# Two groups of attention stages per step on TensorE, and three tiles moved between PSUM banks

## The chip, the core and the metric

The kernel runs on one core of one Trainium2 chip. A core has TensorE (PE, matrix multiplication, and PEld, the loading of its weights), VectorE (DVE), ScalarE (ACT), GpSimd (POOL) and SyncE (SP, which issues the DMAs). Each engine works through its own queue in order and waits on semaphores for the others. TensorE writes into PSUM, which has eight banks; ScalarE and VectorE read it from there. The metric is the time on the device in microseconds, the median of several runs.

## The reference

Linear attention with random features (FAVOR), and then a gated MLP over its output. Eight batches, eight heads, 576 rows, a head size of 64, 128 features; the MLP has 4608 rows, a model width of 512 and an inner width of 1536.

```python
def phi(x):
    proj = einsum('bhsd,md->bhsm', x, omega)
    h = proj - sum(x * x, axis=-1) / 2.0
    h = h - max(h, axis=-1)
    return exp(h) / sqrt(m)
q_p, k_p = phi(q * scale), phi(k * scale)
kv  = einsum('bhsm,bhsd->bhmd', k_p, v)
z   = sum(k_p, axis=2)
num = einsum('bhsm,bhmd->bhsd', q_p, kv)
den = einsum('bhsm,bhm->bhs', q_p, z)[..., None] + 1e-06
x   = (num / den)  # heads side by side: 4608 x 512
g   = x @ w_gate
out = (g / (1 + exp(-g)) * (x @ w_val)) @ w_out
```

## The kernel before, in words

**Attention.** The work is cut into groups of 256 rows of a pair of heads. A group is a block of q or of k, and a step takes two groups: the first six steps take two of k, the next sixty one of q and one of k, the last six two of q, 72 steps (0 to 71). The stages of one group are spread over several steps. `load` (L340) brings q and k three steps ahead. `st_transpose` (L363) turns both groups into the tile `pt` with four TensorE transposes, and ScalarE copies it to `x` (L378), one step ahead. `st_project` (L382) multiplies `x` by omega into two banks, `pp0` and `pp1`. `st_max` (L399) takes the maxima on VectorE (L411 to L414), and `st_exp` (L417) the exponentials on ScalarE, eight instructions (L425), into `ph`. `k_accumulate` (L510) sums k's features times v into `kvacc`, two steps later, in two halves; a sum that is complete is copied to `kvr` (L441), and from batch 4 on its row of denominators is transposed into `zp` (L447). `q_transpose` (L543) turns q's features into `ptq`, copied to `qt` (L554). For batches 0 to 3, `q_mult` (L556) multiplies by `kvr` into `po` and divides by the denominator on VectorE, and `q_out` (L592), three steps behind, transposes the result into `xt`. For batches 4 to 7 the denominators come from GpSimd and VectorE (`q_den`, L471), GpSimd divides the features (`q_norm`, L497), and `q_out` multiplies straight into `xt`. ScalarE and VectorE then split `xt` into a high and a low part, `xh` (L626) and `xl` (L627).

**The MLP** is a generator, `stream` (L683). It goes over 40 visits, each a tile of 512 (or 256) rows of x with a set of three of the twelve blocks of 128 inner columns. A visit is three `g` (L641, 12 matmuls each), then the `o` of the visit before (L650, nine matmuls for each 128 rows), then three `v` (L641). Every product is made of three matmuls from high and low parts. ScalarE applies Silu to `g` (L707), VectorE multiplies by `v` (L721), ScalarE and GpSimd split the result (`hh` L724, `hl` L725), and VectorE adds `o` to the sum (L674). Weights are converted beforehand by another generator, `convert_all` (L247), a `tick` at a time, and loaded again and split for each set (L242, L243).

**The order.** A loop over the steps (L776) calls the eleven stages of `ORDER` (L754). After each stage it gives out some of the MLP, `give(due / left)`, and some ticks of the conversion, so that both keep to a plan: `course` (L191) says how much of the MLP is to be done by which step, within what x allows. The MLP can begin at step `EARLY`, which is 21, when the first two tiles of x are whole. `DENSE` is 35, the step by which all weights are to be converted. The framework then puts the instructions of each engine into a queue by its own estimate of when operands and buffers are ready, earlier emitted work first, and sets the semaphores.

**The banks.** `ps_moe` has four banks for `g`, `v` and `o`; `ps_proj` has two, for `pp0` and `pp1`; `kvacc` has one. The eighth, `ps_att`, is shared in turn by `ptq`, `po`, `xt`, `zp` and, from step 35 on, `pt`; before that `pt` takes a bank of the MLP. In the first 21 steps, which have no MLP work yet, `ptq` and every second `pp` take the MLP's banks too.

Of the kernel before, what the change touches and what calls it, by code (L numbers as in the profile page):

```python
# [23 lines left out]
def kernel(  # L24
# [16 lines left out]
    P = 128  # L41
# [5 lines left out]
    G = 256  # L47
# [23 lines left out]
    OLAG = 3  # L71
# [19 lines left out]
    def ps_att(name, shape):  # L91
        return ps_a.tile(shape, F32, name=name, tag="b")
# [27 lines left out]
    def slots(n, kind):  # L120

        if not 0 <= n < NS:
            return []
        return [(i, b, g, (kgroups if kd == "k" else qgroups)[g]) for i, (kd, b, g) in enumerate(steps[n]) if kd == kind]

    def pairs_of(gr):
        return [(2 * c, 2 * c + 1) for c in range(CH)] if gr is None else [gr[:1]] * CH
# [3 lines left out]
    def column(b, gr):  # L131
        return b * S + (S - RES if gr is None else gr[1])
# [10 lines left out]
    def tile_of(col):  # L143
        j = max(j for j, (c, _) in enumerate(TILES) if c <= col)
        return j, col - TILES[j][0]
# [45 lines left out]
    course = (lower + upper) / 2  # L191
# [8 lines left out]
    EARLY = whole[1]  # L200
# [5 lines left out]
    DENSE = marks[-1][0]  # L206
# [73 lines left out]
    ticks = [0]  # L280

    def tick():
        ticks[0] += 1
        next(wa, None)
# [55 lines left out]
    def load(n):  # L340
        if n >= NS:
            return
        nats[n] = att.tile([P, 2, CH, 2, D], F32, name=f"nat{n}", tag="nat", bufs=3)
        for kind, src in (("q", q), ("k", k)):
            for i, b, _, gr in slots(n, kind):
                load_group(nats[n][:, i], src, b, gr, False)
# [16 lines left out]
    def st_transpose(n):  # L363
        if n >= NS:
            return
        nat = nats.pop(n)
        pt = (ps_moe if n < DENSE else ps_att)(f"pt_{n}", [P, 2, G])
        for i in range(2):
            for c in range(CH):
                nc.tensor.transpose(  # L370
                    pt[:, i, c * P : (c + 1) * P], nat[:, i, c].rearrange("p h d -> p (h d)"), ident
                )
        x = att.tile([P, 2, G], F32, name=f"x_{n}", tag="x")

        st = att.tile([P, 4, 2, CH, 2], F32, name=f"st_{n}", tag="st", bufs=6)
        sq = att.tile([P, 2, CH, 2, D], F32, name=f"sq_{n}", tag="sq")
        nc.gpsimd.tensor_tensor(sq, nat, nat, op=ALU.mult)  # L377
        nc.scalar.copy(x, pt)  # L378
        sts[n] = x, st, sq
        return True  # L380
# [57 lines left out]
    def kv_finalize(b, a2):  # L438
        acc = kvacc.pop((b, a2))
        raw = att.tile([P, 4, VW], F32, name=f"kvr{b}_{a2}", tag="kvr", bufs=4)  # L440
        nc.scalar.copy(raw, acc)  # L441
        for j in range(2):
            kvst[b, 2 * a2 + j] = raw[:, 2 * j : 2 * j + 2, :]
        if b >= BPOOL:

            zp = ps_att(f"zp{b}_{a2}", [4, P])
            nc.tensor.transpose(zp, raw[:, :, D], ident)  # L447
            zs = att.tile([4, P], F32, name=f"zs{b}_{a2}", tag="zs")
            nc.scalar.copy(zs, zp)
            zd = dram.tile([4, P], F32, name=f"zd{b}_{a2}", tag="zd", bufs=4)  # L450
            nc.sync.dma_start(zd, zs)
            zds[b, a2] = zd
# [44 lines left out]
    def q_norm(n):  # L497
        n -= NLAG
        for _, b, g, gr in slots(n, "q"):
            if b < BPOOL:  # L500
                continue
            dn = dns.pop((b, g))
            phv = box["q", b, g].rearrange("p c (h m) -> p (c h) m", m=M)
            nc.gpsimd.tensor_tensor(
                phv, phv,
                dn[:, 2].rearrange("p c (h o) -> p (c h) o", o=1).broadcast_to([P, 2 * CH, M]),
                op=ALU.mult,
            )

    def k_accumulate(n, half):  # L510

        n -= KLAG
        ks = [(b, g, gr, c) for _, b, g, gr in slots(n, "k") for c in range(CH)]
        for b, g, gr, c in ks[half * len(ks) // 2 : (half + 1) * len(ks) // 2]:
            ph, vt = box["k", b, g], vrows[b, g]
            if c == CH - 1:
                busy.remove(vt)
                del box["k", b, g]
            for j, pr in enumerate(pairs_of(gr)[c]):
                a2 = pr // 2  # L520
                first = (b, a2) not in kvacc
                if first:
                    kvacc[b, a2] = ps_k.tile([P, 4, VW], F32, name=f"kvacc{b}_{a2}", tag="kv")
                acc = kvacc[b, a2]
                done.setdefault((b, a2), []).append(pr)
                last = LAST[pr] == (g, c)
                for hh in range(2):
                    nc.tensor.matmul(  # L528
                        acc[:, 2 * (pr % 2) + hh, :],
                        ph[:, c, hh * M : (hh + 1) * M],  # L530
                        vt[:, 2 * c + j if gr is None else c, hh, :],
                        start=first and hh == 0,
                        stop=last,
                        skip_group_check=True,
                    )
                if len(done[b, a2]) == NACC:
                    kv_finalize(b, a2)
        return bool(slots(n, "k"))
# [50 lines left out]
    xt = {}  # L589
    cols_done = [0]  # L590

    def q_out(n):  # L592
        n -= OLAG
        for _, b, g, gr in slots(n, "q"):
            po = ps_att(f"xt{b}_{g}", [P, G])
            first = column(b, gr)
            if b < BPOOL:
                xn = xns.pop((b, g))
                for c in range(CH):
                    nc.tensor.transpose(po[:, c * P : (c + 1) * P], xn[:, c].rearrange("p h d -> p (h d)"), ident)  # L600
            else:
                qt = qts.pop((b, g))

                segs = [(pr, pr * RES, RES) for pr in range(NPAIR)] if gr is None else [(gr[0], 0, G)]
                for pr, o, w in segs:
                    for hh in range(2):
                        nc.tensor.matmul(  # L607
                            po[hh * D : (hh + 1) * D, o : o + w], kvst[b, pr][:, hh, 0:D], qt[:, hh, o : o + w],
                            start=True, stop=True, skip_group_check=True,
                        )  # L610
            j, o = tile_of(first)
            if gr is None:
                parts_ = [(po.rearrange("d (r c) -> d r c", c=RES), slice(0, NPAIR), j, o, RES)]
            else:
                cut = min(TILES[j][1] - o, G)
                parts_ = [(po[:, 0:cut], gr[0], j, o, cut)]
                if cut < G:
                    parts_.append((po[:, cut:G], gr[0], j + 1, 0, G - cut))
            for src, pr, j, o, w in parts_:
                if j not in xt:  # L620

                    while j - NXB >= 0 and not finished(j - NXB):
                        assert give(1), "the MLP waits for x, and x for the MLP"
                    xt[j] = [xres.tile([P, NPAIR, T], F32R, name=f"x{e}{j}", tag=f"x{e}") for e in "hl"]
                hi, lo = (t[:, pr, o : o + w] for t in xt[j])
                nc.scalar.copy(hi, src)  # L626
                nc.vector.tensor_tensor(lo, src, hi.bitcast(F32), op=ALU.subtract)  # L627
            if gr is None or gr[0] == NPAIR - 1:
                cols_done[0] = first + (RES if gr is None else G)
        return bool(slots(n, "q"))  # L630
# [23 lines left out]
    def finished(j):  # L654

        return at_visit[0] > last_visit[j]
# [80 lines left out]
    debt = [0.0]  # L737
    given = [0.0]

    def give(us):  # L740
        debt[0] += us
        while debt[0] > 0:
            u = next(ma, None)
            if u is None:
                debt[0] = 0.0
                return False
            debt[0] -= u
            given[0] += u
        return True
# [1 line left out]

    ORDER = (  # L754
        st_project,
        q_norm,
        q_out,
# [5 lines left out]
        lambda n: k_accumulate(n, 1),  # L763
        st_exp,
        q_den,
    )

    for n in range(2):
# [7 lines left out]
    for n in range(NN):  # L776
        load(n + LA)
        load_v(n + LAV)
        want = OPS * np.interp(clock[n + 1], [clock[m] for m, _ in marks], [x for _, x in marks])
        for i, what in enumerate(ORDER):  # L780
            left = len(ORDER) - i
            what(n)
            due = course[n + 1] - given[0] - debt[0]
            if due > 0:
                give(due / left)
            for _ in range(int(np.ceil((want - ticks[0]) / left))):
                tick()
        load_z(n)
    for _ in ma:
        pass  # L790
# [30 lines left out]
```

## Time and profile before

| what | value |
|---|---|
| median of three runs | 1264.08 us (1259.43 to 1271.75) |
| the profiled execution | 1261.98 us |
| its span from the first to the last instruction | 1260.2 us |
| mean granted clock of TensorE | 0.986 |
| TensorE busy | 1222.5 us (97%) |
| ScalarE, VectorE, GpSimd busy | 632.5, 526.1, 506.2 us |
| first MLP matmul, last transposed x | about 107 and 1035 us |

The page of a profile gives each engine's busy time; a group of instructions by line, operation and tile; and what an engine waited for. `xl<-xt,xh` means that an instruction writes tile `xl` from `xt` and `xh`. A wait is written as the waiting engine, line and tile, an arrow, and the one that released it. Matmuls overlap, so the time that one costs is read from the distance between two starts and not from its duration. The granted clock is the share of TensorE's full clock that it was given.

### The profile page before, as it was taken

What the parts mean: (1) busy time and instruction counts of PE and PEld (TensorE: products, weight loads), DVE (VectorE), ACT (ScalarE), POOL (GpSimd) and SP (SyncE); (2) the same over time, 40 slices, a digit from 0 to 9 for tenths busy, and PEclk for the clock granted to TensorE, in tenths of its full rate; (3) what the DMA queues carried; (4) which work ended last, traced back from release to release, by engine and by line L of the source; (5) the groups of instructions that cost most, each with busy time, mean ns of one, the idle gap of its engine ahead of it and who ended that gap; (6) DMA issues with size and microseconds to landing.
All of it is one profiled execution on the core that took longest, in us unless ns stands there. A gap on an engine that the chain in (4) does not pass through costs nothing.

```text
span 1260.2 us, 19027 instructions
## 1 busy us (share of the span) xinstructions
PE 1222.5 (97%) x7137; PEld 1004.1 (80%) x7137; DVE 526.1 (42%) x1080; ACT 632.5 (50%) x1368; POOL 506.2 (40%) x448
## 2 busy tenths in 40 slices
PE   6999999999899999999999999999999999999998
PEld 5888878888688878877777777877777778888887
DVE  4886795557732343334433433223343311121112
ACT  4887857564444645555556644853644323221211
POOL 3344444445442212644544334444654314242421
PEclk7999999999999999999999999999999999999999
DMA  6656555344521222222212221221211111010112
GB/s 161 152 139 154 141 146 172 106 137 122 159 67 52 61 65 60 76 67 62 65 51 67 68 59 38 64 65 45 52 50 30 39 25 50 25 51 25 51 30 55
DMA packets 157692, 97.80 MB, mean 78 GB/s; under 512 B 119680, under 2 KB 132000, under 8 KB 157600
## 3 DMA queue, kind: packets, MB, share of 16 engines
q1 hardware_dynamic: 157600, 96.59, 28.7%
q8 instruction: 56, 0.92, 0.3%
q14 instruction: 36, 0.29, 0.1%
HBM read 77.66 MB, written 18.89 MB: 77 GB/s over the span
## 4 chain that ended last, share of the span: by engine, by line
PE 67%; DVE 2%; POOL 2%; issue 1%; ACT 1%; DMA 0%; POOLq 0%; ACTq 0%
PE o L650 20%; PE g L641 19%; PE v L641 17%; PE pp L393 3%; PE kvacc L528 2%; PE ptq L552 2%; PE pt L370 2%; PE xt L607 1%; POOL jk L488 1%; PE po L569 1%; ACT ph L425 1%; DVE st L411 1%; DVE dj L492 0%; POOL wlo L243 0%; POOL hl L725 0%
## 5 line engine op out<-in xcount | busy, mean ns | idle before, releaser
L725 POOL TENSOR_TENSOR hl<-sl,hh 128x512 fp32r<-128x512 f32 (+1 forms) x120 | 145.3, 1211 | 223.0 <-ACT hh L724 222.9
L243 POOL TENSOR_TENSOR wlo<-wraw,whi 128x512 fp32r<-128x512 f32 x108 | 138.5, 1294 | 146.1 <-ACT whi L242 135.4
L425 ACT ACTIVATE ph<-pp,st 128x128 f32<-128x128 f32 x576 | 167.7, 387 | 57.7 <-DVE st L414 56.9
L641 PE MATMUL g<-xh,whi 128*128 128x512 f32 (+1 forms) x480 | 185.4, 387 | 0.0
L641 PE MATMUL v<-xh,whi 128*128 128x512 f32 (+1 forms) x480 | 184.3, 384 | 0.0
L641 PE MATMUL g<-xh,wlo 128*128 128x512 f32 (+1 forms) x480 | 179.8, 375 | 0.0
L641 PE MATMUL v<-xh,wlo 128*128 128x512 f32 (+1 forms) x480 | 179.3, 374 | 0.0
L641 PE MATMUL g<-xl,whi 128*128 128x512 f32 (+1 forms) x480 | 179.2, 373 | 0.0
L641 PE MATMUL v<-xl,whi 128*128 128x512 f32 (+1 forms) x480 | 178.5, 372 | 0.0
L650 PE MATMUL o<-whi,hh 128*128 128x512 f32 x432 | 176.5, 408 | 0.6 <-DVE sl L721 0.6
L650 PE MATMUL o<-whi,hl 128*128 128x512 f32 x432 | 169.9, 394 | 1.1 <-POOL hl L725 0.6
L650 PE MATMUL o<-wlo,hh 128*128 128x512 f32 x432 | 170.3, 394 | 0.0
L724 ACT CAST hh<-sl 128x512 fp32r<-128x512 f32 (+1 forms) x120 | 70.0, 583 | 174.5 <-DVE sl L721 174.1
L721 DVE TENSOR_TENSOR sl<-v,sl 128x512 f32<-128x512 f32 (+1 forms) x120 | 76.2, 635 | 172.2 <-PE v L641 167.9
L674 DVE TENSOR_TENSOR acc<-o,acc 128x512 f32<-128x512 f32 x108 | 74.1, 689 | 174.2 <-PE o L650 173.9
L377 POOL TENSOR_TENSOR sq<-nat 128x512 f32<-128x512 f32 x72 | 76.8, 1067 | 155.6 <-DMA nat<-in_k_dram 127.4
L411 DVE TENSOR_REDUCE st<-pp 128x4 f32<-128x512 f32 x144 | 93.5, 683 | 77.2 <-PE pp L393 77.1
L242 ACT CAST whi<-wraw 128x512 fp32r<-128x512 f32 x108 | 66.6, 622 | 97.3 <-PE v L641 55.3
L641 PEld LDWEIGHTS g<-xh,whi 128*128 128x128 f32 x480 | 91.6, 191 | 19.3 <-issue 4.2
L641 PEld LDWEIGHTS v<-xh,whi 128*128 128x128 f32 x480 | 91.0, 189 | 17.5 <-issue 2.7
L641 PEld LDWEIGHTS g<-xh,wlo 128*128 128x128 f32 x480 | 91.5, 191 | 15.9 <-issue 0.4
L641 PEld LDWEIGHTS v<-xh,wlo 128*128 128x128 f32 x480 | 91.0, 190 | 16.0 <-issue 0.5
(67 smaller groups left out, 1910.8 us busy)
## 6 DMA issues: line engine op xcount, KB each, us to landing
wraw<-wscr SPq DMA_DIRECT2D x108, 256.0 KB, 2.7
wscr<-wc SPq DMA_DIRECT2D x36, 256.0 KB, 2.3
out_dram<-acc SPq DMA_DIRECT2D x72, 128.0 KB, 2.3
nat<-in_k_dram SPq DMA_DIRECT2D x64, 128.0 KB, 3.2
v<-in_v_dram SPq DMA_DIRECT2D x64, 128.0 KB, 2.9
nat<-in_q_dram SPq DMA_DIRECT2D x64, 128.0 KB, 2.7
st<-in_moe_w_gate_dram SPq DMA_DIRECT2D x12, 512.0 KB, 4.2
st<-in_moe_w_val_dram SPq DMA_DIRECT2D x12, 512.0 KB, 4.6
```

The source lines that it names most:

```text
L242: nc.scalar.copy(hi, raw)
L243: nc.gpsimd.tensor_tensor(lo, raw, hi.bitcast(F32), op=ALU.subtract)
L377: nc.gpsimd.tensor_tensor(sq, nat, nat, op=ALU.mult)
L393: nc.tensor.matmul(pp[hh][:, i, c, :], x[r, i, c * P : (c + 1) * P], omT[r], start=True, stop=True)
L411: nc.vector.tensor_reduce(st[:, 1, :, :, hh], pp[hh], axis=AX.X, op=ALU.max, negate=True)
L425: nc.scalar.activation(ph[:, c, hh * M : (hh + 1) * M], pp[hh][:, i, c, :], AF.Exp, bias=st[:, 3, i, c, hh : hh + 1], scale=1.0,)
L641: nc.tensor.matmul(ps, a_[:, ws], b_[:, c, :], start=n == 0, stop=n == 3 * NC - 1)
L650: nc.tensor.matmul(ps, a_[:, ts_], b_, start=first and n == 0, stop=last and n == 2)
L674: nc.vector.tensor_tensor(a_, po, a_, op=ALU.add)
L721: nc.vector.tensor_tensor(h, pv, h, op=ALU.mult)
L724: nc.scalar.copy(hh, h)
L725: nc.gpsimd.tensor_tensor(hl, h, hh.bitcast(F32), op=ALU.subtract)
```

## The change

Three things. From step 21 on the loop goes by a new list, `GROUPED`, with two groups of stages: first the projection, the transposition of q's features, both halves of k's sum, the maxima, the exponentials and the denominators; then, a place earlier than before, the normalisation of the next step, the transposition of the next step's q and k, `q_out` and `q_mult`. Behind each group stand three marks `SHARE`, and only there work of the MLP and of the conversion is given out, a sixth of the step's at each. Up to step 20 the order is the old one (`CLOSE`). From step 22 on, `pt` takes a bank of `ps_proj`, and not of the MLP or `ps_att`. From step 21 on, `xt` takes one too, and not `ps_att`.

```diff
-        pt = (ps_moe if n < DENSE else ps_att)(f"pt_{n}", [P, 2, G])
+        pt = (ps_moe if n <= EARLY else ps_proj)(f"pt_{n}", [P, 2, G])
...
-            po = ps_att(f"xt{b}_{g}", [P, G])
+            po = (ps_att if n + OLAG < EARLY else ps_proj)(f"xt{b}_{g}", [P, G])
...
-    ORDER = (
+    SHARE = None
+    CLOSE = (
         st_project,
         q_norm,
         q_out,
...
         st_exp,
         q_den,
     )
+    GROUPED = (
+        st_project,
+        q_transpose,
+        lambda n: k_accumulate(n, 0),
+        lambda n: k_accumulate(n, 1),
+        st_max,
+        st_exp,
+        q_den,
+        SHARE,
+        SHARE,
+        SHARE,
+        lambda n: q_norm(n + 1),
+        lambda n: st_transpose(n + 1),
+        q_out,
+        q_mult,
+        SHARE,
+        SHARE,
+        SHARE,
+    )
...
-        for i, what in enumerate(ORDER):
-            left = len(ORDER) - i
-            what(n)
-            due = course[n + 1] - given[0] - debt[0]
-            if due > 0:
-                give(due / left)
-            for _ in range(int(np.ceil((want - ticks[0]) / left))):
-                tick()
+        order = CLOSE if n < EARLY else GROUPED
+        left = len(order) if n < EARLY else order.count(SHARE)
+        for what in order:
+            if what is not SHARE:
+                what(n)
+            if n < EARLY or what is SHARE:
+                due = course[n + 1] - given[0] - debt[0]
+                if due > 0:
+                    give(due / left)
+                for _ in range(int(np.ceil((want - ticks[0]) / left))):
+                    tick()
+                left -= 1
```

## The prediction

> **What bounds the kernel now.** I read the page first, then TensorE's waits split at the two ends of the changed stretch (107 to 1042 us: the MLP's first matmuls, and the last transposed x), then the clock around the longest waits, then the order of TensorE's instructions around single bursts of attention work.
>
> The page's first part:
>
> ```profile
> span 1260.2 us, 19027 instructions
> PE 1222.5 (97%) x7137; PEld 1004.1 (80%) x7137; DVE 526.1 (42%) x1080; ACT 632.5 (50%) x1368; POOL 506.2 (40%) x448
> ```
>
> TensorE is the bound: 97% busy, nobody else over half. So a gain can only be time in which TensorE waits, runs at a lower clock, or loses something on changing between kinds of work. The waits of TensorE, from 107 to 200 us (first row) and from 200 to 1042 us (second row); the columns are total, times, longest:
>
> ```profile
> PE po L569 <- DVE xl L627: 4.7, 6, 1.9
> PE pt L370 <- DVE xl L627: 11.7, 8, 6.0
> ```
>
> Both name one cause. `pt`, `ptq`, `po` and `xt` take turns in the single bank of `ps_att`, and after `xt` the bank is free only when VectorE's L627 has read it. Two of these waits, as TensorE's timeline has them (the bracket is the idle time):
>
> ```profile
> 114.77 1.08 PE L569 MATMUL po<-kvr,qt 128*128 128x65 f32 x8 [1.93 <-DVE xl L627]
> ...
> 343.17 1.11 PE L370 MATMUL pt<-ident,nat 128*128 128x128 f32 x4 [6.00 <-DVE xl L627]
> ```
>
> A wait costs more than its length. The stretches behind the four longest, with TensorE's busy time first and the granted clock (the column after POOL's) behind:
>
> ```profile
> 116.00:120.00 4.00, 4.00 (x25) 4.00 (x23) 3.49 (x10) 2.53 (x5) 1.59 (x2) 0.57 0.27 60
> 178.00:182.00 4.00, 4.00 (x16) 3.32 (x16) 3.77 (x8) 1.84 (x8) 2.48 (x2) 0.61 0.36 119
> 342.00:349.00 7.00, 5.83 (x18) 4.50 (x20) 1.71 (x4) 3.11 (x9) 3.81 (x3) 0.54 0.51 142
> 628.00:632.00 4.00, 4.00 (x16) 3.39 (x15) 1.05 (x3) 1.20 (x2) 1.25 (x3) 0.57 0.30 68
> ```
>
> Busy time times what is missing to the full clock: 4.00 x 0.43 + 4.00 x 0.39 + 5.83 x 0.46 + 4.00 x 0.43 = 7.7 us lost to the clock.
>
> **The change part by part.** The sum starts from the profiled execution, 1261.98 us, which lies 2.1 us below the median of the three runs (1264.08).
>
> *The banks.* From step 22 `pt`, and from step 21 `xt`, leave the one bank; only `ptq`, `po` and the eight `zp` stay there, half a step apart. The waits of `pt` and `po` on `xl` lose their cause: -4.7 - 11.7 = -16.4 us, and the clock behind them, -7.7 us. Not all of this need be gained: what is late next is under "new waits".
>
> The Trainium skill, "TensorE: Matmul & The Clock Gate", section "Why this matters for your kernels", asks for no idle gap of TensorE over about 3 us, since an idle window of that order brings back the half clock. By that rule only the wait of 6.00 us would cost clock, the second term would be -2.7 us, and the sum 1253.9 us. The trace disagrees: 0.57 follows a wait of 1.93 us (114.77 us, above). I go by the trace.
>
> *Fewer bursts.* Attention work now falls between MLP matmuls in bursts:
>
> ```profile
> 604.01 0.40 PE L641 MATMUL g<-xh,wlo 128*128 128x512 f32 x1
> 604.33 1.16 PE L393 MATMUL pp<-omT,x 64*128 64x128 f32 x16
> 605.42 0.50 PE L641 MATMUL g<-xh,whi 128*128 128x512 f32 x1
> 605.76 0.39 PE L641 MATMUL g<-xl,whi 128*128 128x512 f32 x1
> ...
> 608.05 0.39 PE L641 MATMUL g<-xh,wlo 128*128 128x512 f32 x1
> 608.37 0.65 PE L607 MATMUL xt<-qt,kvr 128*64 128x256 f32 x4
> 608.96 0.50 PE L650 MATMUL o<-whi,hh 128*128 128x512 f32 x1
> 609.29 0.39 PE L650 MATMUL o<-wlo,hh 128*128 128x512 f32 x1
> 609.52 0.39 PE L650 MATMUL o<-whi,hl 128*128 128x512 f32 x1
> 609.75 0.40 PE L650 MATMUL o<-whi,hh 128*128 128x512 f32 x1
> 609.99 0.39 PE L650 MATMUL o<-wlo,hh 128*128 128x512 f32 x1
> 610.22 0.60 PE L370 MATMUL pt<-ident,nat 128*128 128x128 f32 x4
> 610.58 0.48 PE L650 MATMUL o<-whi,hl 128*128 128x512 f32 x1
> ```
>
> Undisturbed MLP matmuls start 0.23 us apart (609.29 to 609.52). Around `pp` three starts lie 605.76 - 604.01 = 1.75 us apart, so this burst costs 1.75 - 2 x 0.23 = 1.29 us; `xt` costs 609.29 - 608.05 - 0.46 = 0.78 us. Where the two stand together:
>
> ```profile
> 589.27 0.39 PE L641 MATMUL v<-xh,wlo 128*128 128x512 f32 x1
> 589.59 1.16 PE L393 MATMUL pp<-omT,x 64*128 64x128 f32 x16
> 590.68 0.65 PE L607 MATMUL xt<-qt,kvr 128*64 128x256 f32 x4
> 591.27 0.50 PE L641 MATMUL v<-xh,whi 128*128 128x512 f32 x1
> 591.60 0.39 PE L641 MATMUL v<-xl,whi 128*128 128x512 f32 x1
> ```
>
> they cost 591.60 - 589.27 - 0.46 = 1.87 instead of 2.07 us: a joint saves 0.2 us at most. `pt`, `ptq` and `kvacc` fill the array and enter at the usual 0.23 us (609.99 to 610.22), so their joints save little. Over the 54 steps 21 to 74, at 0 to 0.2 us a step, it is 0 to 11 us, less what stands together already; I take 4 us.
>
> *New waits in the projections' banks.* Now `pt` of the next step waits until the exponentials have read `pp0`, `xt` until they have read `pp1`, and the next `pp` until `pt` is copied (L378) and `xt` split (L626, L627). Behind a stalled `pt` on TensorE's queue stand `xt`, `po` and the MLP's second half. The cover of this wait is the rest of the first group and half the MLP of a step. From the planner's `course` in the code I work out the MLP's work of a step: 4.1 us in steps 21 to 29, 26.7 in 30 to 35, 9.2 in 36 to 43, 11.5 in 44 to 60, 15.0 in 61 to 73. The rest of the first group is `ptq` and eight `kvacc`, at 0.36 us for each four (610.22 to 610.58): 1.1 us. So the cover is 5.7, 6.9 and 8.6 us in the last three stretches. What it must cover, twice:
>
> ```profile
> 508.89 1.16 PE L393 MATMUL pp<-omT,x 64*128 64x128 f32 x16
> 512.07 2.17 ACT L425 ACTIVATE ph<-pp,st 128x128 f32<-128x128 f32 x8 [1.24 <-DVE st L414]
> ...
> 619.21 1.16 PE L393 MATMUL pp<-omT,x 64*128 64x128 f32 x16
> 626.66 0.43 ACT L425 ACTIVATE ph<-pp,st 128x128 f32<-128x128 f32 x1
> ```
>
> From the end of `pp` to the end of the eight exponentials it is 514.24 - 510.05 = 4.2 us undisturbed and 627.09 - 620.37 = 6.7 us where ScalarE does other things between. The change puts `st_max` and `st_exp` ahead of the step's MLP work, so I expect the short one more often. The long one is late by 1.0 us in steps 36 to 43, 8 us together, and not from 44 on. Bounds: 0, and the 47 us of the second rival; I take 8, by the long row, to which real steps with Silu between are nearest.
>
> *Steps 22 to 30* have no such cover (half of 4.1 us plus 1.1), and the loop itself may rule:
>
> ```profile
> 152.39 2.06 PE L393 MATMUL pp<-omT,x 64*128 64x128 f32 x16
> 155.13 0.59 ACT L378 COPY x<-pt 128x512 f32<-128x512 f32 x1
> 160.16 0.96 PEld L393 LDWEIGHTS pp<-omT,x 64*128 64x128 f32 x8 [0.36 <-ACT ph L425]
> ```
>
> The next `pp` already waits for the exponentials here (last row); a step takes 160.16 - 152.39 = 7.8 us. The change adds `pt` (0.36 us) and the copy (0.59) to this loop, with the hand-overs and the split of `xt` up to 1.6 us a step: 14 us over nine steps. Against it, exponentials that stand ahead of the MLP and of the weights' conversion end sooner. Bounds 0 and 14, I take 6.
>
> *Moved work at nothing or nearly.* `q_norm` (POOL) moves from the start of the next step to the second group; its input comes from `q_den`, half a step earlier, and `q_transpose` needs it half a step later, so half the MLP hides it on both sides; without that cover it would hold up `ptq`. The MLP's and the conversion's DMAs on SP's queue, the weight splits on ACT and POOL and the output stores come in six lumps rather than eleven; the loads of q, k and v stay at the start of a step, and TensorE waited for none of the others after 107 us. The two `k_accumulate` now touch. At the five remainder groups of steps 27 to 63 the second half needs the bank that the first half's sum leaves through `kvr`:
>
> ```profile
> PE kvacc L528 <- ACT kvr L441: 0.5, 1, 0.5
> ```
>
> That was 0.5 us once with work between; 5 x 0 to 1 us, I take 1.
>
> Sum: 1261.98 - 16.4 - 7.7 - 4 + 8 + 6 + 1 = 1248.9 us.
>
> **The rivals.** *The waits only change their name.* `xl` was late because ScalarE and VectorE were; the exponentials run there too. At the longest wait:
>
> ```profile
> 342.70 0.41 DVE L627 TENSOR_TENSOR xl<-xt,xh 128x256 fp32r<-128x256 f32 x1
> 343.34 1.39 ACT L425 ACTIVATE ph<-pp,st 128x128 f32<-128x128 f32 x5
> ```
>
> The old bank came free at 343.11 us, the exponentials ended at 344.73: `pt` in a projection's bank would have waited longer. Against it: these exponentials stood last but one in their step and now stand ahead of the MLP. If it holds, -16.4 - 7.7 comes back in full: about 1262 us (1253 to 1272).
>
> *The second group comes too early* (slower). Its place is `pt` in steps 36 to 60; it decides when the chain from `pp` to the last exponential exceeds the cover of 5.7 and 6.9 us. ScalarE's Silu work can push it there:
>
> ```profile
> L707 ACT ACT_TABLE_LOAD x49 | 62.9, 1283 | 12.9 <-PE g L641 12.2
> L707 ACT ACTIVATE sl<-g 128x512 f32<-128x512 f32 x96 | 57.1, 597 | 61.9 <-PE g L641 56.5 <-POOL hl L725 4.1 <-POOL sq L377 0.7
> ```
>
> Three Silu, a table for them and one back for Exp make 4.2 + 3 x 0.6 + 2 x 1.28 = 8.6 us: 2.9 us late in 8 steps and 1.7 in 17, 52 us. If it hits every second step, 26 us and, at 1.7 us of clock behind each of 12, about 47 us in the place of the 8: 1288 us. Against it: ScalarE is 50% busy, and work that stands earlier in the code tends to run first.
>
> *The groups are dissolved.* In the rows above `pt` stands after five of nine `o` matmuls that the code emits in one piece: the framework moves work by its own estimate of readiness. If it spreads the groups again, the 4 us of joints are not gained, the banks still count: 1253 us.
>
> **How the numbers follow.** Forecast 0.45 (own range 1230 to 1262), dissolved 0.10, renamed waits 0.25, too early 0.20. About 1% (12.6 us) is what a measurement can tell from no change: the three runs spread from 1259.43 to 1271.75. Faster than 1251.4: 0.39 + 0.04 + 0.05 = 0.48; slower than 1276.7: 0.17 of "too early" and 0.06 of "renamed", 0.23; within: 0.29. The forecast is 1248.9, called 1249. The low end takes both unknown costs at 0 and the joints at 7 us, 1231; the high end reaches to half of "too early", 1278.
>
> **What would show it.** Right: no wait of `pt` or `po` on `xl` after 120 us, a clock of 1.00 from 200 us on, `pp`, `ptq` and `kvacc` in one burst. Wrong: waits of `pt` or `xt` on ACT's L425 over 10 us in total after 200 us (rivals one or two, by their size); steps 22 to 30 longer than the 93 us from 107 to 200 by more than 6; a stretch of the granted clock at half speed more often than the present four times; waits of `o` or `g` on Silu, which I priced at nothing.

## The result, and the profile after

| | before | changed |
|---|---|---|
| median | 1260.34 us (11 runs) | 1252.38 us (11 runs) |
| ratio, 95% interval | | 0.9922 (0.990 to 0.9944) |
| profiled execution, its span | 1261.98, 1260.2 us | 1254.07, 1252.3 us |
| first MLP matmul to last matmul, in the profile | 1148.4 us | 1136.2 us |
| changes from MLP to attention work on TensorE | 285 | 149 |
| half-clock stretches after 107 us, together | 17.1 us | 10.2 us |

The change moves two tiles to other banks, `pt` and `xt`, not three. It gains 0.8%, clear of noise and just under 1%. In three runs against the kernel before (two of them below) the ratio was 0.9917 to 0.9931. The two profiles differ by 7.9 us in span, but by 12.2 us from the first MLP matmul on: the first 110 us, where both programs run the same instructions, took 3.9 us more in the profile after. In other profiles of unchanged starts they took 1 to 3 us more than before, or 10 to 11 where the clock was raised only at 51 us and not at 31 to 33. So I compare the stretch from the first MLP matmul to the last one.

The page's first lines after, to be held against those of before:

```profile
span 1252.3 us, 19047 instructions
PE 1217.5 (97%) x7137; PEld 1013.1 (81%) x7137; DVE 530.8 (42%) x1080; ACT 599.4 (48%) x1344; POOL 506.3 (40%) x448
```

TensorE is still the bound. ScalarE is busy 33 us less; I come back to this. TensorE's waits of 0.5 us and more in total, from 107 to 1045 us:

```profile
PE pt L370 <- ACT ph L425: 3.2, 3, 1.3
PE o L650 <- ACT hh L724: 2.8, 1, 2.8
PE v L641 <- DVE acc L674: 2.7, 1, 2.7
PE o L650 <- POOL hl L725: 2.4, 4, 1.3
PE g L641 <- DVE sl L721: 1.7, 1, 1.7
...
PE po L569 <- DVE xl L627: 0.8, 1, 0.8
PE pp L393 <- ACT x L378: 0.5, 1, 0.5
```

The waits of `pt` (11.7 us) and of `po` (4.7 us) on `xl` have shrunk to 0.8 us. New are waits of the MLP itself: `o`, `v` and `g`, 9.6 us, where before there were three of `o`, 1.7 us together.

One step on TensorE (first group, and the second group of the step before):

```profile
749.15 0.39 PE L650 MATMUL o<-whi,hl 128*128 128x512 f32 x1
749.38 0.60 PE L370 MATMUL pt<-ident,nat 128*128 128x128 f32 x4
749.91 0.65 PE L607 MATMUL xt<-qt,kvr 128*64 128x256 f32 x4
750.49 0.50 PE L641 MATMUL v<-xh,whi 128*128 128x512 f32 x1
750.83 0.39 PE L641 MATMUL v<-xl,whi 128*128 128x512 f32 x1
...
755.84 0.39 PE L641 MATMUL v<-xh,wlo 128*128 128x512 f32 x1
756.16 1.16 PE L393 MATMUL pp<-omT,x 64*128 64x128 f32 x16
757.25 0.66 PE L552 MATMUL ptq<-ident,ph 128*128 128x128 f32 x4
757.75 1.00 PE L528 MATMUL kvacc<-v,ph 128*128 128x65 f32 x8
758.56 0.48 PE L641 MATMUL v<-xh,whi 128*128 128x512 f32 x1
758.88 0.39 PE L641 MATMUL v<-xl,whi 128*128 128x512 f32 x1
```

The groups stand as written. By the reckoning of the prediction (less two MLP starts of 0.23 us) the second costs 750.83 - 749.15 - 0.46 = 1.22 us and the first 758.88 - 755.84 - 0.46 = 2.58 us.

The chain from the projection to the exponentials, an ordinary step after:

```profile
680.31 1.16 PE L393 MATMUL pp<-omT,x 64*128 64x128 f32 x16
683.98 2.17 ACT L425 ACTIVATE ph<-pp,st 128x128 f32<-128x128 f32 x8
```

and one of the long ones before, with Silu's table (L707) between:

```profile
701.18 1.16 PE L393 MATMUL pp<-omT,x 64*128 64x128 f32 x16
704.69 1.40 ACT L425 ACTIVATE ph<-pp,st 128x128 f32<-128x128 f32 x5 [1.69 <-DVE st L414]
706.11 1.28 ACT L707 ACT_TABLE_LOAD   x1
```

After, all eight exponentials come in one piece, 686.15 - 681.47 = 4.7 us behind `pp`; that is the median of steps 36 to 70, and the longest is 6.5. Before, the median was 5.9 and the longest 16.1, since Silu came between and each change of function loads a table. There were 97 table loads before and are 73 now: 24 x 1.28 = 31 us of ScalarE's time, though ScalarE is not the bound.

### The profile page after: what moved, and what is told of

Its sections match the earlier page's. It is cut to its first block, busy times and chain, and to the rows that moved or that the text cites. A ratio compares the mean times of both kernels' runs of the same rounds, so it can differ in the third digit from the quotient of the medians.

```text
span 1252.3 us, 19047 instructions
## 1 busy us (share of the span) xinstructions
PE 1217.5 (97%) x7137; PEld 1013.1 (81%) x7137; DVE 530.8 (42%) x1080; ACT 599.4 (48%) x1344; POOL 506.3 (40%) x448
## 4 chain that ended last, share of the span: by engine, by line
PE 68%; DVE 2%; POOL 1%; ACT 1%; issue 0%; DMA 0%; SPq 0%; POOLq 0%; DVEq 0%
PE o L650 19%; PE g L641 19%; PE v L641 19%; PE pp L393 3%; PE kvacc L528 2%; PE ptq L552 2%; PE xt L607 2%; PE pt L370 1%; PE po L569 1%; POOL hl L725 1%; DVE st L266 0%; DMA nat<-in_k_dram 0%; DVE sl L721 0%; ACT ph L425 0%; DVE st L411 0%
## 5 line engine op out<-in xcount | busy, mean ns | idle before, releaser
L725 POOL TENSOR_TENSOR hl<-sl,hh 128x512 fp32r<-128x512 f32 (+1 forms) x120 | 142.3, 1190 | 208.0 <-ACT hh L724 207.9
L641 PE MATMUL g<-xh,whi 128*128 128x512 f32 (+1 forms) x480 | 181.6, 379 | 1.7 <-DVE sl L721 1.7
L641 PE MATMUL v<-xh,whi 128*128 128x512 f32 (+1 forms) x480 | 180.1, 375 | 2.7 <-DVE acc L674 2.7
L650 PE MATMUL o<-whi,hh 128*128 128x512 f32 x432 | 173.4, 401 | 2.8 <-ACT hh L724 2.8
L425 ACT ACTIVATE ph<-pp,st 128x128 f32<-128x128 f32 x576 | 157.9, 384 | 32.8 <-DVE st L414 32.5
L721 DVE TENSOR_TENSOR sl<-v,sl 128x512 f32<-128x512 f32 (+1 forms) x120 | 75.7, 633 | 181.3 <-PE v L641 179.3
```

Of the source, the lines that this page charges most:

```text
L425: nc.scalar.activation(ph[:, c, hh * M : (hh + 1) * M], pp[hh][:, i, c, :], AF.Exp, bias=st[:, 3, i, c, hh : hh + 1], scale=1.0,)
L641: nc.tensor.matmul(ps, a_[:, ws], b_[:, c, :], start=n == 0, stop=n == 3 * NC - 1)
L650: nc.tensor.matmul(ps, a_[:, ts_], b_, start=first and n == 0, stop=last and n == 2)
L721: nc.vector.tensor_tensor(h, pv, h, op=ALU.mult)
L725: nc.gpsimd.tensor_tensor(hl, h, hh.bitcast(F32), op=ALU.subtract)
```

## The experiments

All times are medians with the kernel before run beside them; ratios are to that kernel. What the profiles say is gathered here: the stretch from the first to the last MLP matmul, the changes from MLP to attention work in it, and from 107 us on the sum of TensorE's waits and the length of the half-clock stretches. Rows of waits are from 107 to 1045 us unless another stretch is named.

| kernel | median, us | ratio | stretch | changes | waits | half clock |
|---|---|---|---|---|---|---|
| before | 1260.3 | 1 | 1148.4 | 285 | 19.4 | 17.1 |
| changed | 1252.4 | 0.9922 (0.990 to 0.9944) | 1136.2 | 149 | 15.6 | 10.2 |
| after_again | 1250.6 | 0.9917 (0.9895 to 0.9939) | 1134.2 | 149 | 14.5 | 10.2 |
| after_side | 1251.2 | 0.9931 (0.9906 to 0.9956) | 1134.2 | 149 | 13.9 | 10.2 |
| banks_only | 1284.1 | 1.0191 (1.0153 to 1.0228) | 1167.8 | 259 | 40.1 | 23.9 |
| exp_first_old_banks | 1282.2 | 1.0171 (1.014 to 1.0202) | 1168.5 | 267 | 36.3 | 17.1 |
| spread_exp_first | 1272.2 | 1.0089 (1.0069 to 1.0108) | 1157.2 | 248 | 21.1 | 20.5 |
| one_group | 1253.3 | 0.9948 (0.9926 to 0.997) | 1138.1 | 151 | 16.5 | 13.7 |
| groups_pt_old | 1255.5 | 0.995 (0.993 to 0.997) | 1140.3 | 151 | 16.9 | 20.5 |
| ticks_spread | 1254.1 | 0.9952 (0.9931 to 0.9974) | 1136.9 | 150 | 14.0 | 17.1 |
| x_early | 1259.2 | 0.998 (0.9967 to 0.9993) | 1140.1 | 153 | 28.1 | 13.7 |
| both | 1262.4 | 1.001 (0.9993 to 1.0028) | 1149.3 | 154 | 29.7 | 30.7 |
| late_hybrid | 1250.5 | 0.9912 (0.9894 to 0.9931) | 1134.8 | 160 | 19.1 | 3.4 |
| late_split | 1247.5 | 0.9883 (0.9855 to 0.9912) | 1128.8 | 153 | 14.1 | 3.4 |

### The changed kernel again (after_again, after_side)

No edit.

> The changed kernel once more, unchanged, to see what of its profile comes again. If the waits of `o` on `hh` (2.8 us at 763 us), of `v` on `acc` (2.7 us at 359 us) and of `g` on `sl` (1.7 us at 342 us) belong to the order of the queues, they stand at the same places within 0.5 us each. If they are accidents of one execution, they go or move. The start up to the first MLP matmul, which the change does not touch and which took 3.4 us longer than in the profile before (step 20's projection at 106.0 instead of 102.6 us), should differ again by a few us if it is chance. Ratio to the kernel before 0.990 to 0.995.

> The changed kernel beside the other three of this call, for their comparison: ratio to before 0.990 to 0.994.

The waits from 200 to 1042 us in after_again:

```profile
PE o L650 <- ACT hh L724: 2.8, 1, 2.8
...
PE g L641 <- DVE sl L721: 2.2, 1, 2.2
```

The MLP's new waits come again at the same places, that of `o` to a tenth of a microsecond; `v` on `acc`, 2.7 us above, is 1.2 here and 1.0 in after_side, further off than the 0.5 us expected. So they belong to the order of the queues, though not in every length. The half-clock stretches come elsewhere in part: at 511 and 767 us in the first profile, at 342 and 762 us in both repeats. The start was chance: step 21's projection starts at 113.1 and 112.7 us in these two, at 114.8 in the first profile and at 110.9 before.

### One part alone: the banks (banks_only)

```diff
-        order = CLOSE if n < EARLY else GROUPED
+        order = CLOSE
```

with MLP work again behind every stage.

> The old order of the stages in all steps, with the new banks for pt and xt. Now xt and pt stand right behind the projection in whose banks they go, ahead of the exponentials that free them. If the banks alone make the gain, ratio to before 0.98 to 0.99 and no wait of pt or po on xl. If the gain needs half the MLP's work between the groups, pt and xt wait on the exponentials (L425) in most of the 54 steps, 1 us or more each unless the framework puts MLP work ahead of them, and the time is 20 to 60 us above before, ratio 1.015 to 1.05.

From 107 to 1045 us:

```profile
PE xt L600 <- ACT ph L425: 16.8, 9, 7.2
PE xt L607 <- ACT ph L425: 13.1, 8, 2.9
```

The banks alone lose 1.9%. `xt` has left the bank where it waited for copies, and waits in the projections' for the exponentials, which in the old order end 6.0 us (median) and up to 15 us behind `pp`. This is the rival "the waits only change their name", and worse; it holds for the old order.

### Early exponentials with the old banks (exp_first_old_banks)

The kernel before, with from step 21 on:

```diff
         st_project,
+        st_max,
+        st_exp,
         q_norm,
...
-        st_max,
         q_transpose,
         lambda n: k_accumulate(n, 1),
-        st_exp,
         q_den,
```

> The kernel before, banks included, with one edit: from step 21 on st_max and st_exp stand right behind st_project. If the old waits of pt and po on xl came only from ScalarE's late and broken-up exponentials, they fall from 16.4 us to under 5 and the ratio to before is 0.985 to 0.993, and the new banks were not needed. If they came from four tiles taking turns in one bank, 10 us or more of these waits stay and the ratio is 0.996 to 1.005.

```profile
PE pt L370 <- DVE xl L627: 11.9, 11, 2.1
PE ptq L552 <- DVE xn L579: 6.0, 5, 3.0
PE po L569 <- DVE xl L627: 5.4, 6, 2.4
```

The ratio lies above both expected ranges. The waits of `pt` and `po` on `xl` stay, 17.3 us, and others join: early exponentials do not relieve the one bank. So ScalarE's late exponentials alone were not the cause; four kinds of tiles in turn in one bank are what is left, as the prediction read it. Of the four, groups_pt_old and x_early (below) point to `xt`. The stretch grew by 20 us over before and the waits by 17, most of them of `ptq` and `pt`; why the earlier exponentials bring these is open.

### The groups' order without groups (spread_exp_first)

```diff
     GROUPED = (
         st_project,
         q_transpose,
-        lambda n: k_accumulate(n, 0),
-        lambda n: k_accumulate(n, 1),
         st_max,
         st_exp,
+        lambda n: k_accumulate(n, 0),
         q_den,
-        SHARE,
-        SHARE,
-        SHARE,
+        lambda n: k_accumulate(n, 1),
         lambda n: q_norm(n + 1),
         lambda n: st_transpose(n + 1),
         q_out,
         q_mult,
-        SHARE,
-        SHARE,
-        SHARE,
     )
```

with MLP and conversion work behind every stage.

> From step 21 on the eleven stages stand apart again, with MLP work behind each, but in the order of the two groups: the maxima and exponentials early, the transposition of the next step's q and k, q_out and q_mult last; banks as in the changed kernel. Theory 'place of the exponentials': what the banks need is that the exponentials are ahead of the MLP's work and pt and xt late; the two groups add only fewer joints, 0.1 us in each of 54 steps. Then the chain from the projection to the last exponential stays at 4.7 us in the median after step 36, no wait on xl, and the time is 2 to 7 us above the changed kernel, ratio to before 0.993 to 0.998. Theory 'groups': without the groups the gain is gone, with waits on the exponentials of 10 us or more, ratio 1.0 or above.

```profile
PE pp L393 <- DVE xl L627: 4.2, 5, 1.7
PE ptq L552 <- ACT qt L554: 4.1, 1, 4.1
```

Theory "groups" is nearer: the gain is gone and 0.9% lost, though not by waits on the exponentials, which come to 1.3 us. The first theory was not tried in full: the chain from the projection to the last exponential is 5.8 us in the median of steps 36 to 70, and not 4.7. The waits are spread over `pp`, `ptq`, `zp` and `o`. Against the changed kernel's repeats the stretch is 23 us longer. Of that, waits make 7 us and half clock about 5 us; some 11 us I cannot place, among them whatever the 99 more changes of work cost.

### No MLP work between the groups (one_group)

```diff
         q_den,
-        SHARE,
-        SHARE,
-        SHARE,
         lambda n: q_norm(n + 1),
```

so that six marks stand behind both groups.

> The changed kernel with the second group moved straight behind the first, and all six marks behind both. This takes away the cover of half the MLP's work (4.6 to 7.5 us) and keeps the banks. The chain from the projection to the last exponential is 4.7 us in most steps; without cover pt waits 4.7 - 1.1 = 3.6 us in each of 50 steps, 180 us, if the framework keeps the order, ratio to before 1.10 to 1.15 with the clock. If the framework moves MLP work ahead of pt by its own estimate, most of this does not come: ratio 0.99 to 1.02.

It keeps most of the gain, 0.9948 against 0.9917 to 0.9931, with overlapping intervals. TensorE's attention work in one step (MLP matmuls between the rows left out):

```profile
469.86 1.16 PE L393 MATMUL pp<-omT,x 64*128 64x128 f32 x16
470.95 0.66 PE L552 MATMUL ptq<-ident,ph 128*128 128x128 f32 x4
471.44 1.00 PE L528 MATMUL kvacc<-v,ph 128*128 128x65 f32 x8
472.57 1.00 PE L569 MATMUL po<-kvr,qt 128*128 128x65 f32 x8
...
476.68 0.60 PE L370 MATMUL pt<-ident,nat 128*128 128x128 f32 x4
```

The framework itself leaves 4.2 us between `kvacc` and `pt` here, and 3.8 us in the median of steps 36 to 65: it moves `po` and MLP matmuls ahead of `pt`, which starts 1.0 us (median) behind the last exponential that reads its bank rather than 2.5. Other waits come for it, above all 5.8 us of `po` on `qt`. The half of the MLP written between the groups is a margin, not the condition on which the gain hangs.

### Where pt goes (groups_pt_old)

```diff
-        pt = (ps_moe if n <= EARLY else ps_proj)(f"pt_{n}", [P, 2, G])
+        pt = (ps_moe if n < DENSE else ps_att)(f"pt_{n}", [P, 2, G])
```

> The two groups, xt in the projections' banks, but pt where it was: an MLP bank up to step 34, the one bank of ps_att from then on. If the move of pt is what removed its waits, pt or po waits again for the one bank, mostly on ScalarE's copy of ptq or on VectorE's read of po, 3 us or more in total after 200 us, and the ratio to before is 0.994 to 1.0. If the move of xt alone was enough (xl was the releaser of all these waits), no such wait comes, and the time is that of the changed kernel within 3 us, ratio 0.990 to 0.995; the loop of steps 22 to 30 is then without pt and its copy, and that stretch (89.6 us from step 21's to step 30's projection) 3 to 8 us shorter.

```profile
PE po L569 <- ACT x L378: 4.7, 1, 4.7
```

One wait in the shared bank, now on `pt`'s own copy, the half clock behind it, and 0.995. Of the waits on `xl` in that bank only the 0.8 us of `po` before 200 us stands, as in the changed kernel: so `pt`'s move is not what removed them. Steps 21 to 29 took 87.1 us without `pt` in the loop, and 89.6, 89.3 and 89.5 with it, but held 178 MLP matmuls instead of 185, which is 1.6 us. Up to step 36, where both kernels have 994, this one is 2.2 to 2.7 us shorter when waits and half clock are taken off (an estimate), below the 3 to 8 expected. The intervals of this kernel and the changed one overlap; the profiled wait speaks for the move of `pt`.

### The new waits of the MLP: late x or lumps of conversion

Two theories. "Late x": since `q_out` stands in the second group, the next tile of x is whole half a step later in the order, and where the plan runs at the limit of x the MLP has nothing to do, or must do `o` right behind `v`. "Lumps": the conversion, at six marks instead of eleven, blocks VectorE's queue ahead of the MLP's instructions.

x_early:

```diff
     GROUPED = (
+        q_out,
         st_project,
-        q_transpose,
         lambda n: k_accumulate(n, 0),
         lambda n: k_accumulate(n, 1),
+        q_transpose,
...
         lambda n: st_transpose(n + 1),
-        q_out,
         q_mult,
...
-            po = (ps_att if n + OLAG < EARLY else ps_proj)(f"xt{b}_{g}", [P, G])
+            po = ps_att(f"xt{b}_{g}", [P, G])
```

The edit also puts `q_transpose` behind both halves of k's sum.

> q_out stands first in the first group, and its xt stays in the bank of ps_att; all else as in the changed kernel. Theory 'late x': since q_out stands in the second group, the MLP's next tile of x is whole half a step later, and where the plan runs at its limit (steps 44 and 60) the first half of a step has no MLP work or puts o right behind v. Then the wait of o on hh at 763 us, the missing MLP work in step 44 and the two half-clock stretches behind them go: 4.4 us of waits, about 1.3 us in step 44 and 4.8 us of clock, so 8 to 10 us faster than the changed kernel, ratio to before 0.983 to 0.987. Theory 'lumps' (the waits come from conversion and MLP work given out in six lumps): these waits stay, same time as the changed kernel within 3 us, ratio 0.990 to 0.995. If xt in the one bank brings the old waits of pt or po on xl back, po waits on xl again, 4 us or more.

The waits from 200 us on:

```profile
PE ptq L552 <- DVE xl L627: 12.7, 7, 5.3
```

With `xt` in the one bank the old wait is back, with `ptq` in the place of `pt`, and eats the gain; a new wait of `xt` on `xn`, 6.9 us before 200 us, adds to it. From step 40 to 71 the kernel took 513.3 us, less than the 517.5, 515.5 and 515.6 us of the changed one.

ticks_spread:

```diff
+        places = len(order)
...
-                for _ in range(int(np.ceil((want - ticks[0]) / left))):
-                    tick()
                 left -= 1
+            for _ in range(int(np.ceil((want - ticks[0]) / places))):
+                tick()
+            places -= 1
```

> The weights' conversion is given out behind each of the seventeen places of the list and not only at the six marks; the MLP as in the changed kernel. Theory 'lumps': the waits of v on acc at 359 us and of g on sl at 342 us go, since fewer conversion instructions stand together on VectorE's queue ahead of them: 4.5 us faster than the changed kernel, ratio to before about 0.988. Theory 'late x': nothing changes at 763 us, where the conversion is over, and the rest stays within 2 us: ratio 0.990 to 0.994. Rival: the conversion comes between the projection and the exponentials again, which lengthens their chain from 4.7 us (median after step 36, where there is no conversion left, so only steps 21 to 35 can lose): up to 6 us slower.

```profile
PE g L641 <- DVE sl L721: 4.3, 1, 4.3
```

`v` waits for 0.5 us only, but `g` waits longer (1.7 to 2.2 us in the changed kernel), and the time is the same or a little worse. In this profile finer lumps only move the wait.

both (the two edits):

> x_early and ticks_spread together. If both theories hold and the two causes are independent, 12 to 14 us faster than the changed kernel, ratio to before 0.979 to 0.984. If only late x holds, as x_early; if only lumps, as ticks_spread.

The two do not add: 1.001, with 16.0 us of `ptq` on `xl` after 200 us.

late_hybrid (x_early's order and bank from step 40 on only):

```diff
+    LATE = 40
...
+        order = CLOSE if n < EARLY else GROUPED if n < LATE else GROUPED_LATE
```

> The changed kernel up to step 39; from step 40 on, where the weights' conversion is over, the order and xt's bank of x_early. From x_early's profile: its stretch from step 40 to 71 took 513.3 us, that of the changed kernel 517.6 and 515.5 in its two profiles, while its loss lay before step 40, where ptq waited on xl for 5.3 us at once. So 2 to 4 us faster than the changed kernel, ratio to before 0.987 to 0.990, steps 44 to 46 in 33 instead of 35 to 36.5 us. If ptq's waits on xl come back after step 40 (7.4 us of them stood there or before in x_early), it is no faster than the changed kernel.

0.9912 beside 0.9931 of after_side: no difference that these runs can tell. Steps 44 to 46 took 32.8 us, as expected. The half clock fell to 3.4 us, and 4.6 us of `ptq` on `xl` took its place.

late_split (from step 44 on):

```diff
+    LATE = 44
+    GROUPED_LATE = (
+        q_out,
+        st_project,
+        lambda n: k_accumulate(n, 0),
+        lambda n: k_accumulate(n, 1),
+        st_max,
+        st_exp,
+        q_den,
+        SHARE,
+        SHARE,
+        SHARE,
+        lambda n: q_norm(n + 1),
+        lambda n: st_transpose(n + 1),
+        q_transpose,
+        SHARE,
+        SHARE,
+        SHARE,
+    )
...
-            po = (ps_att if n + OLAG < EARLY else ps_proj)(f"xt{b}_{g}", [P, G])
+            po = (ps_proj if EARLY <= n + OLAG < 44 else ps_att)(f"xt{b}_{g}", [P, G])
```

> The changed kernel up to step 43. From step 44 on, with only batches 4 to 7 left for q: q_out stands first in the first group with xt in the bank of ps_att, and q_transpose moves to the second group, half a step behind it, so that ptq no longer follows xt in that bank at once. Theory 'late x': the missing MLP work of step 44 and half of the waits at 756 to 768 us go, and ptq does not wait on xl (4.6 us in late_hybrid): 3 to 6 us faster than the changed kernel, ratio to before 0.986 to 0.990. If the waits of o on hh and hl at 756 to 768 us stay as they are, they come from VectorE's queue (the denominators' L492 ahead of the MLP's L721) and not from the late x, and the gain is at most 3 us, ratio 0.989 to 0.993.

0.9883, the fastest of all, though its interval overlaps those of the changed kernel; its stretch is 5.4 us shorter than the shortest of that kernel. In the changed kernel step 44 had been this on TensorE:

```profile
507.08 0.56 PE L528 MATMUL kvacc<-vrest,ph 128*128 128x65 f32 x4
508.39 0.66 PE L370 MATMUL pt<-ident,nat 128*128 128x128 f32 x4 [0.75 <-ACT ph L425]
508.91 0.44 PE L600 MATMUL xt<-ident,xn 128*128 128x128 f32 x2
509.87 0.71 PE L393 MATMUL pp<-omT,x 64*128 64x128 f32 x4 [0.52 <-ACT x L378]
```

the attention work of two steps with no MLP matmul between, because the plan's next MLP work needed x from that very `q_out`. In late_split 60 MLP matmuls stand in step 44 as before the change. Of its waits from 200 to 1042 us:

```profile
PE o L650 <- POOL hl L725: 2.5, 4, 1.3
PE o L650 <- ACT hh L724: 1.8, 1, 1.8
```

From step 44's to step 46's projection it took 32.9 us, as long as the kernel before; the changed kernel took 36.6 us in its first profile and 35.0 and 34.9 in the repeats, for 108 MLP matmuls each. All four kernels with `q_out` first there took 32.8 to 32.9 us. So the late x cost the changed kernel 2 to 3.6 us there, the larger figure with the half clock behind it; late_split's whole 5 us hold also the clock (3.4 us of half clock in the place of 10.2) and the move of `ptq`, which were not tried apart. The wait of `o` on `hh` only fell from 2.8 to 1.8 us, and that on `hl` stayed, so that neither clause of the expectation holds whole: these waits mostly stay, and the gain is still more than 3 us. In the changed kernel the wait on `hh` arose so:

```profile
761.50 0.17 DVE L414 SCALAR_TENSOR_TENSOR st<-st 128x8 f32<-128x8 f32 x1
764.22 0.69 DVE L492 TENSOR_REDUCE dj<-jk 128x4 f32<-128x512 f32 x1 [2.56 <-POOL jk L488]
764.82 0.68 DVE L721 TENSOR_TENSOR sl<-v,sl 128x512 f32<-128x512 f32 x1
...
765.54 0.62 ACT L724 CAST hh<-sl 128x512 fp32r<-128x512 f32 x1 [1.67 <-DVE sl L721]
...
766.21 0.50 PE L650 MATMUL o<-whi,hh 128*128 128x512 f32 x1 [2.82 <-ACT hh L724]
```

VectorE stood idle for 2.56 us before L492, a sum of the denominators that waits for GpSimd, and GpSimd for the exponentials; behind it stood the MLP's product L721, on which `hh` and `o` wait, though the last of its `v` matmuls had ended at 761.57 us. This reading, that the denominators ahead in the queue are the cause, was not tried by itself.

## Why the prediction was right or wrong

The time, 1252.4 us, lies in the range, 3.4 us above the forecast. The gain was put at 15 us from the median then shown and is 8 us by the later medians, 8 to 11 over the repeats; within 1% of no change, which had a chance of 0.29 where "faster" had 0.48. Within the profiles, from the first MLP matmul on, it is 12.2 us, and 14.2 in both repeats, against 13.1 forecast; the agreement is in part luck, since terms were off in both directions. Of the 12.2 us, waits make 3.8 (19.4 to 15.6) and the clock 3.2 (TensorE was busy for 15.4 us of the old half-clock stretches and for 9.0 of the new, at half speed). The other 5.2 us are more than I can place below.

**The banks' waits: right.** -16.4 us forecast, -15.6 measured. exp_first_old_banks shows that late exponentials alone are not the cause; the waits on `xl` stay away with only `pt` back in the one bank (groups_pt_old) and return with `xt` (x_early, where `q_out` moved too). banks_only shows that the cure needs the groups' order. The groups with both old banks were not run.

**The clock: too high.** -7.7 us forecast. The old half-clock stretches after 107 us, 17.1 us, are gone from their places, but others of 10.2 us stand behind new waits and the first profile's step 44, so some 3 us are left of the term. The full clock from 200 us on, a sign of being right, did not come.

**The joints: smaller, as far as shown.** 4 us put. A step's attention work costs 2.58 + 1.22 = 3.80 us. Apart, in the profile before, it is 1.29 + 0.78 (the prediction's `pp` and `xt`), 0.43 each for `ptq` and `pt` and 0.45 for each half of `kvacc` (medians of steps 44 to 70 by the same reckoning), together 3.83. Over 54 steps that is 1.6 us. Whether the 5.2 us above hold more of this term is open.

**New waits in the projections' banks: too high.** 8 us put; `pt` on L425 came to 1.9 us after 200 us, and `pp` on `x` to 0.5. The chain was 4.7 us in the median, between the prediction's two rows (4.2 and 6.7), and longer than the smallest cover of 5.7 us in three of the 35 steps from 36 on.

**Steps 22 to 30: too high.** 6 us put. From step 21's to step 30's projection it took 89.5 us before and 89.6 after, but with 178 and 185 MLP matmuls. Up to step 36, where both have 994, it took 288.8 and 282.5 us: 6.3 us less, while waits fell by 2.4 us and the half clock that vanished was worth 6.0 (half of TensorE's busy time in it). So the longer loop took back about 2 us. The step of 7.8 us in the prediction was a short one; the nine steps' mean was 9.9.

**Moved work at nothing: wrong.** This is the step that failed. It put the MLP's DMAs, the weight splits and the output stores in six lumps at nothing, as well as waits of `o` or `g` on Silu, and 1 us for `kvr`, of which no wait came. The MLP's own waits rose from 1.7 to 9.6 us, with 6.8 us of half clock behind the longest. I looked at which engine has time left, and not at what stands ahead of the MLP's instruction in its queue. For the longest wait the trace shows the denominators there; that the six lumps cause the others is not shown (ticks_spread). The late x, 2 to 3.6 us, was not in the sum at all: `q_out` moved by half a step, and the plan that tells the MLP when x is whole was not moved with it.

**The rivals.** "The waits only change their name" holds for the banks without the groups (banks_only), not for the change. Its time was mis-summed: with 16.4 and 7.7 us back in full the prediction's own sum is 1273 us, and not 1262. "Too early" did not come: `pt` waited for the exponentials twice after 200 us, 1.9 us together, and the written cover matters less than I argued, as one_group shows. The groups were not dissolved.

## What to carry to other kernels

When a tile moves to another bank, ask which instruction frees that bank and where this one stands in the order; the banks and the order here are worth 0.8% together, and the banks alone cost 1.9%. When a stage is moved in a written order, look at every plan that assumes when its result is there: half a step of late x left one step without MLP work, at 2 to 3.6 us. Price the work that is "moved at nothing" by what is queued ahead of it, since an engine that is 42% busy held TensorE up for 2.8 us.

## What the hardware showed that I had not expected

The clock falls by windows, and beside attention work a short wait can be enough. Starts of half-clock stretches before lie 163.9 and 286.7 us apart (177.7, 341.6, 628.3 us), 48 and 84 times 3.413 us. The windows just ahead, with TensorE's busy time first and the granted clock behind POOL's column, in the kernel before:

```profile
174.29:177.70 3.41, 1.83 (x12) 1.32 (x11) 3.41 (x9) 1.13 (x4) 0.43 (x1) 1.00 0.98 256
177.70:181.10 3.40, 3.40 (x14) 3.01 (x14) 3.17 (x6) 1.62 (x7) 2.48 (x2) 0.50 0.22 79
```

and in the changed one:

```profile
357.40:360.80 3.40, 2.30 (x11) 1.57 (x9) 3.37 (x5) 0.00 (x0) 3.06 (x2) 1.00 0.20 77
360.80:364.20 3.40, 1.83 (x8) 1.53 (x9) 3.28 (x6) 0.00 (x0) 1.30 (x1) 1.00 0.32 99
504.20:507.60 3.40, 3.40 (x38) 3.18 (x34) 1.92 (x5) 1.76 (x6) 0.00 (x0) 1.00 0.00 0
507.60:511.00 3.40, 2.13 (x13) 1.59 (x13) 1.34 (x4) 2.77 (x9) 1.82 (x2) 1.00 0.41 92
511.00:514.40 3.40, 3.40 (x10) 2.64 (x9) 0.02 (x1) 0.00 (x0) 1.53 (x2) 0.50 0.24 50
```

The wait of 2.67 us at 359 us fell across two windows, and the clock stayed full. In the window from 507.6 us TensorE waited only 1.3 us, and was busy 2.13 of 3.4 us, more than the 1.83 us of the window from 360.8 us, but mostly with small attention matmuls: the clock halved. The window from 504.2 us, full of attention work without a wait, kept the clock. In both repeats the same step 44, with the same waits, fell otherwise across the windows (busy 3.14 and 2.38 us, and 2.77 and 2.75), and the clock stayed full. In all fourteen profiles every fall after 107 us comes at the edge of such a window, and TensorE was busy for at most 2.3 us of the window ahead of it; but a window with 1.5 us, of MLP work alone, kept the clock (banks_only, from 670.3 us). So the price of a wait depends on where it falls and on what else is in its window. The Trainium skill, "TensorE: Matmul & The Clock Gate", section "Part 1: The HAM clock gate", tells of a free-running window of 3413 ns; the distances above agree. The rule that the Trainium skill gives on the same page, section "Why this matters for your kernels", no gap over about 3 us, does not carry here: 1.3 us of waiting was enough beside attention work. That attention matmuls count for less than MLP matmuls is a guess from these windows, and was not tried by itself.
